# Reordering the first batch's front in an attention + token-mixing + MLP kernel on one Trainium2 core

## The chip, the cores and the metric

The kernel runs on one core of a Trainium2 chip. A core has a matrix engine (PE, with its weight loads shown apart as PEld), a vector engine (DVE), a scalar engine (ACT), a general engine (POOL), and a queue engine (SP) that here only issues DMAs. Each engine works through its own list of instructions in order and waits on semaphores for the others. Data lives in SBUF, and PE writes into eight PSUM banks of 128 x 512 f32. The metric is the time on the device of one execution in microseconds (us); lower is better. One execution was also recorded by the hardware profiler; all durations below are from that trace, counted from its start.

## The reference, cut to what matters

Chunked attention over B=4 batches, H=8 heads, S=768 tokens of D=64, then one block that mixes tokens with a low-rank pair U, V and channels with a two-layer MLP:

```python
def _attn_ref(q, k, v, mem_k, mem_v):            # chunk, left_ctx, right_ctx = 32, 16, 8; n_mem = 8
    for c in range(S // chunk):
        q_c = q[:, :, c*32 : c*32+32]
        k_full, v_full = memory rows + rows max(0, c*32-16) : min(S, c*32+40) of k, v
        scores = (q_c @ k_full.T) / sqrt(D)
        a = exp(scores - max);  a = a / (sum(a) + 1e-9)
        out[:, :, chunk] = a @ v_full

def _moe_ref(x, U, V, w_ch1, w_ch2):             # x: (4, 768, 512); U: (768, 32); V: (32, 768)
    h = x.transpose(0, 2, 1) @ U @ V
    u = x + h.transpose(0, 2, 1)
    return u + np.maximum(u @ w_ch1, 0.0) @ w_ch2   # w_ch1: (512, 2048), w_ch2: (2048, 512)
```

U, V, w_ch1 and w_ch2 arrive as float64, read on chip as pairs of 32-bit words.

## The kernel before

The kernel works batch by batch. A batch's attention runs in three parts, T = 0, 1, 2, each of 256 tokens: two token tiles `xs[(b, 2T)]` and `xs[(b, 2T+1)]` of 128 tokens x 512 channels. After attention the token mixing and the MLP of a batch run on PE in steps (`w1_step`, `w2_step`), and the next batch's attention is woven between them. Batch 0 has nothing to be woven into: its attention, the decoding of U, V and of the first slice of w_ch1 and the first half of its token mixing make up the **front**, roughly the first 47 us, and the first MLP step can't begin before it is over.

In the front the order of every engine's instructions is the order in which the Python code of `attention(0, ...)` writes them; a planner orders what comes later. Its pieces, with the line numbers of the profile:

- `q_part(T, h)` and `k_main(T, h, ...)` copy turned queries and keys into place on ACT (L694, L672 to L678). `s_turn(T)` makes a part's scores with 64 small matmuls (L714) in two banks.
- `s_weights(T)` takes, for each bank, the maximum (L736), the difference (L737), both on DVE, and the exponential on ACT (L740). `s_sums(T)` sums the rows (L745, two), adds 1e-9 (L749) and takes the reciprocal (L750), all on DVE: the normalization.
- `t_part(T, s)` turns the weights on PE (four matmuls, L768), and ACT copies them out of PSUM (L771). `av_part(T)` multiplies by v with 64 small matmuls (L788) into two banks, and DVE then writes the part's two token tiles with four products (L800).
- `collect(t)` adds U'x of token tile t to one PSUM bank, `gp[0]` (L812, one matmul with 512 columns in f32). `turn_x` turns token tiles 0, 1, 2 for all four column blocks (L1152, 12 matmuls) into four banks, two of the pool `ps_h` and the accumulators `acc0` and `acc1`. `turn_x1` does so later for tiles 3 to 5 (L1176).
- `Words` decodes float64 words: `begin` on ACT (L238), then `shift` (L245), `low` (L253, L258) and `join` (L265) on DVE. `u_words` is for U (its result goes to `u3` on DVE, L907, and to `u_sb` on POOL, L911), `v_words` for V. `spread_v` spreads V over partitions on PE (L290, 3 matmuls); ACT casts it (L295) and DVE subtracts (L296). `advance(5)`, behind it, decodes the first slice of w_ch1 (ACT L238; DVE L245 to L265), which therefore stands ahead of the last part's products L800 on DVE.
- `bank()` hands out PSUM banks in a cycle (`cyc`) over the pools `ps_a` (3 buffers), `ps_h` (2) and two accumulators while `wide[0]` is a number, and from `ps_a` alone once it is None. `keep_clock(n)` puts n matmuls of a zero tile `busy` (512 columns, L141) ahead of the next use of a bank; the program begins with 12 of them.
- `take(len(loading))`, behind `av_part(1)`, issues the loads of the last v rows and of the first slices of w_ch1 and w_ch2 on SP.

Of the kernel before, what the change touches and what calls it, by code (L numbers as in the profile page):

```python
# [25 lines left out]
HEAD = {ET.Activation, ET.Pool}  # L26
FIRST = 3000
START = 12
PROBS = [5, 0, 9]
LOADS = 'mv t1 t2 uv v0 v1 v2 a0 b0 w1 w2'  # L30
WLO = 4
# [27 lines left out]
def chunk_attn_then_mixer_kernel(  # L59
# [73 lines left out]
            return ps_h.tile([P, 512], F32, name="ps_h")  # L133
        return ps_o.tile([P, 512], F32, name="acc" + kind[1])

    warm = [0]

    def att_ps():
        ps = bank()
        for _ in range(warm[0]):  # L140
            nc.tensor.matmul(out=ps, lhsT=busy[:, 0:P], rhs=busy, start=True, stop=True)  # L141
        warm[0] = 0
        return ps

    def keep_clock(n):

        warm[0] += n

    busy = slot([P, 512], BF16, "busy")
    nc.vector.memset(busy, 0.0)  # L150
# [373 lines left out]
    def attention(b, xs):  # L524
# [141 lines left out]
        def k_main(T, h, psv):  # L666
            copy = nc.scalar.copy
            m, w = NM // 2, CK // 2
            kt = kall[:, NB * (T % 2):NB * (T % 2) + NB].rearrange("c i p (n r) -> c p r i n", r=2)
            for q_ in range(2):  # L670
                p = 2 * h + q_
                copy(out=kt[:, p, :, :, m:m + w], in_=psv[:, q_])  # L672
                copy(out=kt[:, p, :, 0:NB - 1, m + w:], in_=psv[:, q_, :, 1:, 0:NW // 2 - m - w])
            p = slice(2 * h, 2 * h + 2)
            if T == 0:
                copy(out=tail[:, p].rearrange("c p (n r) -> c p r n", r=2), in_=psv[:, :, :, 0, 0:LEFT // 2])
            if T == NP - 1:
                copy(out=kall[:, NB * (T % 2) + NB - 1, p, NM + CK:NM + CK + LEFT], in_=tail[:, p])  # L678
# [144 lines left out]
        if b == 0:  # L823
# [32 lines left out]
            take(1)  # L856
            spread_mv(vbs[0])
            take(2)
            keep_clock(START)
            regroup(kraw, kn, "kn", 0)  # L860
            for h in two:
                k_part(0, h)
# [25 lines left out]
            made = [k_edges(2, h) for h in two]  # L888
            for h in two:
                s_weights(0, *sc, [h])  # L890
                k_main(2, h, made[h])
            yield
            sc = s_turn(1)
            for h in two:
                q_part(2, h)
            s_weights(1, *sc)
            s_sums(0)
            u_words.begin()
            yield
            sc = s_turn(2)  # L900
            for s in two:
                t_part(0, s)
            s_weights(2, *sc)
            u_words.shift()
            u_words.low()
            av_part(0)
            nc.vector.tensor_copy(  # L907
                out=u3, in_=u_words.join()[:, 0:NT * R].rearrange("p (t r) -> p t r", t=NT)[:, :, None, :]
                .broadcast_to([P, NT, 3, R]),
            )  # L910
            nc.gpsimd.tensor_copy(out=u_sb, in_=u3[:, :, 0, :])  # L911
            s_sums(1)
            yield
            for s in two:
                t_part(1, s)
            v_words.begin()
            av_part(1)
            take(len(loading))
            for t in range(4):
                collect(t)  # L920
            s_sums(2)
            v_words.shift()
            v_words.low()
            val = v_words.join()
            for s in two:
                t_part(2, s)
            early = turn_x(range(NCK))
            wide[0] = None
            spread_v(val)
            yield  # L930
            advance(5)
            av_part(2)
            yield
            advance(1)
            for t in range(4, NT):
# [208 lines left out]

    def turn_x(cs):

        banks = []
        for c in cs:
            ps = ps_h.tile([P, 512], F32, name="ps_h") if c < 2 else ps_o.tile([P, 512], F32, name=f"acc{c - 2}")
            banks.append(ps)  # L1150
            for tt in range(TB):
                nc.tensor.matmul(  # L1152
                    out=ps[:, tt * P:(tt + 1) * P], lhsT=xs[(0, tt)][:, c * P:(c + 1) * P],
                    rhs=ident, start=(tt == 0), stop=False, skip_group_check=True,
                )
        return banks

    def join_uT(banks, g3):
        uht, ult = u_pair(0, 0)
# [562 lines left out]
```

## Time and profile before

| | us |
|---|---|
| median of 3 runs | 656.05 |
| the runs | 656.5, 656.05, 653.25 |
| the profiled execution | 653.21 |
| its span in the trace | 651.4 |
| PE busy | 620.5 (95% of the span) |
| DVE busy | 381.5 (59%) |
| ACT busy | 252.7 (39%) |

The profiled execution took 653.21 us, its trace spans 651.4 us, so 1.8 us lie outside the trace. The share of busy time is a mean over the whole program. The front has to be read from the timelines of PE, DVE and ACT, in which one row is a run of alike instructions: its start, how long it took, engine, line, operation, and in brackets how long the engine had been idle before it and what it waited for ("issue" means that the trace shows nothing that it waited for). A matmul of f32 data takes two passes, so it shows as two records.

### The profile page before, as it was taken

How to read it: one execution, taken by the hardware profiler on the slowest of the kernel's cores; microseconds unless marked ns; L12 is line 12 of the kernel's file. 1: busy time of each engine (PE TensorE's matmuls, PEld its weight loads, DVE VectorE, ACT ScalarE, POOL GpSimd, SP SyncE). 2: the span in 40 equal slices, each digit the busy share in tenths (PEclk: the TensorE clock that was granted, in tenths of full speed). 3: DMA queues.
4: the chain of work that ended last, by engine and by line, in shares of the span. 5: the costliest groups of instructions: out<-in, count | busy, mean ns of one | idle time of the engine just before them, and what ended most of it. 6: DMA issues, size and time to landing. Idle time of an engine off the chain costs nothing.

```text
span 651.4 us, 15085 instructions
## 1 busy us (share of the span) xinstructions
PE 620.5 (95%) x5992; PEld 537.0 (82%) x5992; DVE 381.5 (59%) x727; ACT 252.7 (39%) x635; POOL 139.2 (21%) x292
## 2 busy tenths in 40 slices
PE   7788999999898999899999999999999999999997
PEld 4557899988786889789889798898877899999886
DVE  6858788798792837953756824653546832222322
ACT  5426445348332445432245713321247712121221
POOL 5100000053153445302634200202315300000000
PEclk9989999999998999899999999999999999999999
DMA  9894586757886699576589949766413056555201
GB/s 244 156 352 176 172 252 226 226 179 177 177 191 163 162 309 297 182 183 157 170 246 206 173 149 263 242 180 181 138 46 116 1 169 187 145 165 160 97 1 48
DMA packets 168705, 115.02 MB, mean 177 GB/s; under 512 B 100956, under 2 KB 139484, under 8 KB 168636
## 3 DMA queue, kind: packets, MB, share of 16 engines
q1 hardware_dynamic: 168012, 113.92, 62.7%
q8 instruction: 47, 0.77, 0.5%
q10 hardware_dynamic: 624, 0.15, 0.1%
q14 instruction: 22, 0.18, 0.1%
HBM read 90.83 MB, written 28.97 MB: 184 GB/s over the span
## 4 chain that ended last, share of the span: by engine, by line
PE 56%; DVE 5%; DMA 3%; ACT 3%; POOL 2%; issue 2%; SPq 2%; ACTq 0%; DVEq 0%; POOLq 0%
PE ps_h L1322 23%; PE acc L1553 16%; PE acc L1563 8%; PE ps_a L788 2%; PE ps_h L1502 2%; DMA blocks<-spread 2%; ACT uc L169 1%; PE acc L1547 1%; DMA w1l<-w1s 1%; POOL pt L169 1%; PE ps_a L714 1%; PE ps_a L818 1%; POOL vb L493 1%; DVE x L1518 1%; DMA w1s<-vb 1%
## 5 line engine op out<-in xcount | busy, mean ns | idle before, releaser
L1553 PE MATMUL acc<-w,hh 128*128 128x512 f32 x612 | 158.3, 394 | 1.3 <-ACT hh L1336 1.3
L1553 PEld LDWEIGHTS acc<-w,hh 128*128 128x128 f32 x612 | 113.9, 189 | 23.1 <-ACT hh L1336 2.8
L1563 PE MATMUL acc<-w,hl 128*128 128x512 f32 x306 | 86.9, 392 | 0.0
L1563 PEld LDWEIGHTS acc<-w,hl 128*128 128x128 f32 x306 | 56.9, 188 | 11.9
L1322 PE MATMUL ps_h<-t12h,w1l 128*128 128x384 f32 x192 | 55.5, 343 | 1.0 <-ACT c L1348 0.7
L1322 PE MATMUL ps_h<-bh,w1l 128*128 128x384 f32 x192 | 53.6, 344 | 0.0
L169 POOL COPY pt<-y 32x128 f32<-32x128 f32 x96 | 30.2, 314 | 99.2 <-DVE y L166 95.0
L1322 PE MATMUL ps_h<-t34h,w1l 128*128 128x384 f32 x152 | 45.9, 343 | 0.2
L1502 PE MATMUL ps_h<-uh,w1h 128*128 128x384 f32 x124 | 42.9, 349 | 2.8 <-ACT w1h L395 1.7
L169 POOL COPY uc<-y 32x128 f32<-32x128 f32 x96 | 32.7, 340 | 56.2 <-DVE y L166 52.5
L1502 PE MATMUL ps_h<-ul,w1h 128*128 128x384 f32 x124 | 41.5, 339 | 0.4 <-DVE ul L1198 0.4
L1337 DVE SCALAR_TENSOR_TENSOR hl<-ps_h,hh 128x384 fp32r<-128x384 f32 x29 | 16.1, 554 | 42.8 <-ACT hh L1336 42.7
L1344 DVE TENSOR_TENSOR c<-ps_h,c 128x384 f32<-128x384 f32 x19 | 10.5, 554 | 48.8 <-PE ps_h L1322 48.8
L1322 PEld LDWEIGHTS ps_h<-t12h,w1l 128*128 128x128 f32 x192 | 35.2, 188 | 4.2 <-issue 1.4
L1337 DVE SCALAR_TENSOR_TENSOR hl<-hst,hh 128x384 fp32r<-128x384 f32 x36 | 20.6, 576 | 29.9 <-PE acc L1563 21.3
L1322 PEld LDWEIGHTS ps_h<-bh,w1l 128*128 128x128 f32 x192 | 35.6, 190 | 0.9 <-issue 0.2
L1322 PE MATMUL ps_h<-b,w1l 128*128 128x384 f32 x174 | 35.5, 339 | 0.3 <-DVE hst L1344 0.3
L1336 ACT ACTIVATE hh<-ps_h 128x384 fp32r<-128x384 f32 x29 | 14.2, 491 | 53.3 <-PE ps_h L1322 53.3
L1344 DVE TENSOR_TENSOR hst<-ps_h,hst 128x384 f32<-128x384 f32 x36 | 19.9, 553 | 24.0 <-ACT hst L1348 16.9
L1336 ACT ACTIVATE hh<-hst 128x384 fp32r<-128x384 f32 x36 | 18.8, 524 | 36.3 <-PE acc L1553 30.0
L1322 PE MATMUL ps_h<-t12l,w1l 128*128 128x384 f32 x96 | 32.3, 337 | 0.0
L575 POOL COPY kn<-kraw 128x512 f32<-128x512 f32 x8 | 8.3, 1039 | 112.5 <-DVE vb L258 102.2
(248 smaller groups left out, 1279.5 us busy)
## 6 DMA issues: line engine op xcount, KB each, us to landing
w1l<-w1s SPq DMA_DIRECT2D x155, 256.0 KB
rw<-in_moe_w_ch_dram SPq DMA_DIRECT2D x14, 512.0 KB
out_dram<-x SPq DMA_DIRECT2D x24, 256.0 KB
blocks<-spread SPq DMA_DIRECT2D x24, 256.0 KB
vb<-in_v_dram SPq DMA_DIRECT2D x56, 98.0 KB
raw<-in_moe_w_ch_dram SPq DMA_DIRECT2D x20, 256.0 KB
rw<-in_moe_w_ch_dram SPq DMA_DIRECT2D x16, 256.0 KB
w1s<-sums SPq DMA_DIRECT2D x16, 256.0 KB
```

Source lines behind the costliest of these rows:

```text
L169: (nc.scalar.copy if both and (5 * to + at) % 8 < 3 else nc.gpsimd.tensor_copy)(out=dst[CK * to:CK * to + CK, :, CK * at:CK * at + CK], in ...
L493: nc.gpsimd.tensor_tensor(out=out, in0=in0, in1=in1, op=op)
L575: (nc.gpsimd if b == 1 or front[0] and T == 2 else nc.vector).tensor_copy(out=groups[T, h].rearrange("n r h d -> n h r d"), in_=raws.pop(( ...
L714: nc.tensor.matmul(out=psv[s][(slice(CK * i, CK * i + CK), t) + ((p // 2, p % 2) if b >= DIRECT else (p % 2, p // 2))], lhsT=qt[p // 2][ro ...
L788: nc.tensor.matmul(out=psv[g][CK * i:CK * i + CK, t, j], lhsT=pt[s][rows, 2 * t + k_, CK * i:CK * i + CK], rhs=vt[rows, NI * t + i, D * j: ...
L1322: nc.tensor.matmul(out=ps[:, :TOK], lhsT=w_, rhs=u, start=(start and m == 0), stop=(m == 5), skip_group_check=True,)
L1336: nc.scalar.activation(out=hh, in_=c, func=AF.Relu)
L1337: nc.vector.scalar_tensor_tensor(out=hl, in0=c, scalar=0.0, in1=hh.bitcast(F32), op0=ALU.max, op1=ALU.subtract,)
L1344: nc.vector.tensor_tensor(out=out, in0=ps[:, :TOK], in1=in1, op=ALU.add)
L1502: nc.tensor.matmul(out=ph[:, :TOK], lhsT=w[:, c, :], rhs=u[c], start=(m == 0), stop=(m + 1 == len(parts)),)
L1553: nc.tensor.matmul(out=acc[tt], lhsT=h[:, sl], rhs=w, start=(begins and m == 0), stop=False,)
L1563: nc.tensor.matmul(out=acc[tt], lhsT=hl[:, sl], rhs=w2h[f], start=False, stop=ends is not None)
```

## The change

Nothing of what is computed changes. In the front of batch 0:

- `u_words.begin` moves on ACT from behind part 0's sums to between the exponential of part 0's first bank and `k_main(2, 0)`; the rest of U's decoding (DVE L245, L253, L258, L265, L907, POOL L911) moves from around `av_part(0)`'s products to behind part 0's two differences, ahead of part 1's first maximum.
- `v_words.begin` takes the place on ACT that `u_words.begin` leaves. The rest of V's decoding moves on DVE from behind part 2's sums to behind part 1's, ahead of `av_part(1)`'s products.
- The four collects 0 to 3, which stood together behind `av_part(1)`, are split: 0 and 1 ahead of `av_part(1)`, 2 and 3 behind it.
- `wide[0] = None` moves ahead of `t_part(2)`, so both of its banks are from `ps_a`.
- `turn_x` goes one token tile at a time (four matmuls): tile 0 ahead of `spread_v`, tile 1 behind it, tile 2 behind `av_part(2)`.
- `keep_clock` takes a width, and ten matmuls of the zero tile with 64 columns (FILL = 10) are put into the first bank of `av_part(2)` ahead of its own.

Lines of the changed kernel are one higher up to `attention`, and eight higher behind `turn_x`; within `attention` they differ by a few.

```diff
+FILL = 10
...
-    warm = [0]
+    warm = []
...
-        for _ in range(warm[0]):
-            nc.tensor.matmul(out=ps, lhsT=busy[:, 0:P], rhs=busy, start=True, stop=True)
-        warm[0] = 0
+        for width in warm:
+            nc.tensor.matmul(out=ps[:, 0:width], lhsT=busy[:, 0:P], rhs=busy[:, 0:width], start=True, stop=True)
+        warm.clear()
...
-    def keep_clock(n):
-        warm[0] += n
+    def keep_clock(n, width):
+        warm.extend([width] * n)
...
-            keep_clock(START)
+            keep_clock(START, 512)
...
             for h in two:
                 s_weights(0, *sc, [h])
+                if h == 0:
+                    u_words.begin()
                 k_main(2, h, made[h])
+            u_words.shift()
+            u_words.low()
+            nc.vector.tensor_copy(
+                out=u3, in_=u_words.join()[:, 0:NT * R].rearrange("p (t r) -> p t r", t=NT)[:, :, None, :]
+                .broadcast_to([P, NT, 3, R]),
+            )
+            nc.gpsimd.tensor_copy(out=u_sb, in_=u3[:, :, 0, :])
             yield
...
             s_sums(0)
-            u_words.begin()
+            v_words.begin()
             yield
...
             s_weights(2, *sc)
-            u_words.shift()
-            u_words.low()
             av_part(0)
-            nc.vector.tensor_copy(
-                out=u3, in_=u_words.join()[:, 0:NT * R].rearrange("p (t r) -> p t r", t=NT)[:, :, None, :]
-                .broadcast_to([P, NT, 3, R]),
-            )
-            nc.gpsimd.tensor_copy(out=u_sb, in_=u3[:, :, 0, :])
             s_sums(1)
             yield
             for s in two:
                 t_part(1, s)
-            v_words.begin()
-            av_part(1)
-            take(len(loading))
-            for t in range(4):
+            for t in two:
                 collect(t)
-            s_sums(2)
             v_words.shift()
             v_words.low()
             val = v_words.join()
+            av_part(1)
+            take(len(loading))
+            for t in two:
+                collect(2 + t)
+            s_sums(2)
+            wide[0] = None
             for s in two:
                 t_part(2, s)
             early = turn_x(range(NCK))
-            wide[0] = None
+            next(early)
             spread_v(val)
+            next(early)
             yield
             advance(5)
+            keep_clock(FILL, 64)
             av_part(2)
+            early = next(early)
             yield
...
     def turn_x(cs):
-        banks = []
-        for c in cs:
-            ps = ps_h.tile([P, 512], F32, name="ps_h") if c < 2 else ps_o.tile([P, 512], F32, name=f"acc{c - 2}")
-            banks.append(ps)
-            for tt in range(TB):
+        banks = [
+            ps_h.tile([P, 512], F32, name="ps_h") if c < 2 else ps_o.tile([P, 512], F32, name=f"acc{c - 2}") for c in cs
+        ]
+        for tt in range(TB):
+            for c in cs:
                 nc.tensor.matmul(
-                    out=ps[:, tt * P:(tt + 1) * P], lhsT=xs[(0, tt)][:, c * P:(c + 1) * P],
+                    out=banks[c][:, tt * P:(tt + 1) * P], lhsT=xs[(0, tt)][:, c * P:(c + 1) * P],
                     rhs=ident, start=(tt == 0), stop=False, skip_group_check=True,
                 )
-        return banks
+            yield banks
```

On PE, from the collects behind part 1 to those behind part 2, the kernel before has these rows (`acc_323` is the collects' bank, `dec` V's decoded words):

```order
L812 MATMUL acc_323<-x,uarea 96x512 x4
L768 MATMUL ps_a<-ident,pt 128x128 x4
L768 MATMUL ps_h<-ident,pt 128x128 x4
L1152 MATMUL ps_h<-ident,x 128x128 x6
L1152 MATMUL acc_845<-ident,x 128x128 x3
L1152 MATMUL acc_849<-ident,x 128x128 x3
L290 MATMUL ps_a<-dec,rep 96x256 x3
L788 MATMUL ps_a<-vbe,pt 32x64 x64
L812 MATMUL acc_323<-x,uarea 96x512 x2
```

All four collects, then all 12 turns of tokens (L1152), stand in one piece ahead of `spread_v` (L290). In the changed kernel the same stretch of PE, up to the first of the narrow matmuls, reads:

```order
L813 MATMUL acc_323<-x,uarea 96x512 x2
L769 MATMUL ps_a<-ident,pt 128x128 x8
L1160 MATMUL ps_h<-ident,x 128x128 x2
L1160 MATMUL acc_839<-ident,x 128x128
L1160 MATMUL acc_840<-ident,x 128x128
L291 MATMUL ps_a<-dec,rep 96x256 x3
L1160 MATMUL ps_h<-ident,x 128x128 x2
L1160 MATMUL acc_839<-ident,x 128x128
L1160 MATMUL acc_840<-ident,x 128x128
L142 LDWEIGHTS busy
L142 MATMUL ps_a<-busy 128x64
```

Two collects are gone from here to ahead of `av_part(1)`. Only four of the 12 turns of tokens are left ahead of `spread_v` (L290, now L291), four follow it, and behind them come the ten narrow matmuls (one pair of their rows is shown), `av_part(2)`, the last four turns and collects 4 and 5.

On DVE, from the last product of part 0 to the first two of part 1, the kernel before has (`dec` is here U's words, `pt` the weights, `rs` the reciprocal sums, `x` a token tile):

```order
L800 TENSOR_TENSOR x<-ps_a,rs 128x256
L265 TENSOR_TENSOR dec<-dec 128x192
L907 COPY uarea<-dec 128x576
L745 TENSOR_REDUCE rs<-pt 128x2x2x2 x2
L749 TENSOR_SCALAR rs<-rs 128x16
L750 RECIPROCAL rs<-rs 128x16
L800 TENSOR_TENSOR x<-ps_h,rs 128x256
L800 TENSOR_TENSOR x<-acc_727,rs 128x256
```

The sums (L745) stand behind U's last two steps. On DVE, in the same place, the changed kernel has (`dec` is now V's words, with `vraw` as their source):

```order
L801 TENSOR_TENSOR x<-ps_a,rs 128x256
L746 TENSOR_REDUCE rs<-pt 128x2x2x2 x2
L750 TENSOR_SCALAR rs<-rs 128x16
L751 RECIPROCAL rs<-rs 128x16
L246 TENSOR_SCALAR dec<-dec 96x256
L254 TENSOR_SCALAR dec<-dec 96x256
L259 SCALAR_TENSOR_TENSOR dec<-vraw,dec 96x256
L266 TENSOR_TENSOR dec<-dec 96x256
L801 TENSOR_TENSOR x<-ps_h,rs 128x256
L801 TENSOR_TENSOR x<-acc_733,rs 128x256
```

U's last two steps are gone from between part 0's products and part 1's sums, and V's four stand between those sums and part 1's products. On DVE of the changed kernel, from part 0's last difference to part 1's first maximum, stand:

```order
L738 TENSOR_TENSOR pt<-ps_a,mx 128x512
L246 TENSOR_SCALAR dec<-dec 128x192
L254 TENSOR_SCALAR dec<-dec 128x192
L259 SCALAR_TENSOR_TENSOR dec<-uarea,dec 128x192
L266 TENSOR_TENSOR dec<-dec 128x192
L897 COPY uarea<-dec 128x576
L737 TENSOR_REDUCE mx<-ps_a 128x8
```

Part 1's maximum (L736, now L737) now has U's five steps ahead of it on DVE. On the other engines the moves are those named above; the order of SP's DMAs is unchanged. Behind the front, in the first MLP steps, the order differs at one place on ACT: one Relu (L1510) stands ahead of the cast of the second slice of w_ch2 (L395) and three reads of words (L238), where it stood behind them.

## Rows read from the trace of the kernel before

**Rows 1.** Stretches: us, busy (count) of PE, PEld, DVE, ACT, POOL; clock, DMA share, GB/s.

```profile
0.00:14.00 14.00, 11.44 (x180) 7.38 (x181) 8.82 (x23) 6.77 (x25) 6.63 (x16) 1.00 0.93 260
30.00:35.00 5.00, 5.00 (x70) 2.76 (x59) 4.57 (x14) 0.38 (x1) 0.00 (x0) 1.00 0.79 208
44.00:45.00 1.00, 1.00 (x2) 0.28 (x1) 0.71 (x2) 0.00 (x0) 0.00 (x0) 0.50 1.07 393
80.00:90.00 10.00, 10.00 (x54) 9.24 (x53) 8.98 (x17) 3.23 (x7) 0.00 (x0) 1.00 0.78 242
```

**Rows 2.** Timeline of PE in the front: start, us, operation, idle before and releaser.

```profile
26.88 0.60 PE L768 MATMUL ps_a<-ident,pt 128*128 128x128 f32 x4
29.08 0.21 PE L788 MATMUL ps_h<-vb,pt 64*32 64x64 f32 x1 [0.95 <-issue]
30.48 3.67 PE L812 MATMUL acc<-x,uarea 128*96 128x512 f32 x8
33.99 0.60 PE L768 MATMUL ps_a<-ident,pt 128*128 128x128 f32 x4
34.86 1.82 PE L1152 MATMUL ps_h<-ident,x 128*128 128x128 f32 x12
37.95 0.68 PE L290 MATMUL ps_a<-dec,rep 32*96 32x256 f32 x6
39.58 1.75 PE L788 MATMUL ps_a<-vbe,pt 64*32 64x64 f32 x128 [0.94 <-issue]
43.51 3.64 PE L812 MATMUL acc<-x,uarea 128*96 128x512 f32 x4 [2.18 <-DVE x L800]
46.99 1.28 PE L1176 MATMUL ps_a<-ident,x 128*128 128x128 f32 x10
```

**Rows 3.** Timeline of DVE in the front.

```profile
17.88 0.69 DVE L736 TENSOR_REDUCE mx<-ps_a 128x8 f32<-128x512 f32 x1 [2.08 <-PE ps_h L714]
25.48 0.25 DVE L245 TENSOR_SCALAR dec<-dec 128x192 int32<-128x192 int32 x1
26.48 0.42 DVE L800 TENSOR_TENSOR x<-ps_h,rs 128x256 f32<-128x256 f32 x1
26.82 0.41 DVE L800 TENSOR_TENSOR x<-ps_a,rs 128x256 f32<-128x256 f32 x1
27.81 0.35 DVE L265 TENSOR_TENSOR dec<-dec 128x192 f32<-128x192 f32 x1
28.57 1.27 DVE L745 TENSOR_REDUCE rs<-pt 128x8 f32<-128x512 f32 x2
30.09 0.25 DVE L750 RECIPROCAL rs<-rs 128x16 f32<-128x16 f32 x1
33.58 0.23 DVE L245 TENSOR_SCALAR dec<-dec 96x256 int32<-96x256 int32 x1
34.63 0.42 DVE L265 TENSOR_TENSOR dec<-dec 96x256 f32<-96x256 f32 x1
39.06 1.09 DVE L296 TENSOR_TENSOR v<-ps_a,v 32x256 fp32r<-32x256 f32 x3 [4.01 <-ACT v L295]
42.70 1.42 DVE L800 TENSOR_TENSOR x<-ps_a,rs 128x256 f32<-128x256 f32 x4
```

**Rows 4.** Timeline of ACT in the front.

```profile
18.48 0.68 ACT L694 COPY qt<-ps_a 128x256 f32<-128x256 f32 x2 [0.61 <-PE ps_a L626]
21.19 0.37 ACT L238 ACTIVATE dec<-uarea 128x192 f32<-128x192 f32 x1
39.46 0.44 ACT L238 ACTIVATE dec<-rw 128x256 f32<-128x256 f32 x1
```

**Rows 5.** Timeline of PE: the zero tile's matmuls at the start.

```profile
1.47 4.97 PE L141 MATMUL ps_a<-busy 128*128 128x512 bf16 x12 [1.47 <-DVE kall L200]
```

**Rows 6.** Timeline of PE in the first MLP steps.

```profile
70.24 0.44 PE L1502 MATMUL ps_h<-uh,w1h 128*128 128x384 f32 x1 [0.56 <-ACT w1h L395]
```

**Rows 7.** A piece of the chain that ended last: start, us, what.

```profile
233.40 5.58 DMA blocks<-spread
```

## The prediction

> **What bounds the kernel now.** I read the page first: PE is busy for 95% of the span, so a gain has to come from PE's own idle time or from PE running slowly. The table by stretches came second. In a typical later stretch PE is busy for 10.00 of 10 us [rows 1]. There nothing can be won, but a lead that PE brings into such a stretch is also kept. So I turned to PE's timeline in the front and looked for the brackets, which are the idle times.
>
> The end of the front hangs on a loop between PE and DVE. PE makes weighted values of part 2 at 39.58, but the collects 4 and 5 start only at 43.51, after 2.18 us idle, waiting for DVE's products [rows 2]. DVE's products begin at 42.70 [rows 3], though PE had the values ready from 39.58+1.75 = 41.33 on. DVE was late because it had the subtractions of spread V and w_ch1's words to do first, and before those it sat idle for 4.01 us until PE had spread V [rows 3]. PE spread V at 37.95, behind 12 turns of tokens (34.86 to 37.95) and four collects [rows 2], although V's words had been joined by 34.63+0.42 = 35.05 [rows 3]. So the path is: collects, turns of weights, turns of tokens, spread of V, V's subtractions, w_ch1's words, products, collects. The reader is to see that DVE's queue order makes PE's order at 34 us set the time at 43 us.
>
> A second loss sits at the same place. Collects 4 and 5 take 46.99 - 43.51 = 3.48 us, the four before them 33.99 - 30.48 = 3.51 us [rows 2], so one costs 1.74 instead of 0.88. In that stretch the granted clock is 0.50 [rows 1], the 1.2 GHz level; PE had been idle for 0.94 us, busy for 1.75 and idle for 2.18 before it [rows 2].
>
> **U's words, moved ahead.** They are five steps of DVE, 26.48 - 25.48 = 1.00 us for three and 28.57 - 27.81 = 0.76 for two, together 1.76. They now stand ahead of part 1's first maximum, where DVE sat idle for 2.08 us waiting for scores [rows 3]. They fit with 0.32 to spare, if U has landed. Ahead of U on its queue lie 12 loads of q and k of 256 KB; with U's own 192 KB that makes 3.34 MB. The first 14 us moved 260 GB/s, or 3.64 MB [rows 1], so I estimate that U is there at about 13 us; the latest the trace allows is 21.19, when ACT read it [rows 4]. On ACT the read (0.37) now stands ahead of `k_main(2)`. ACT has 0.61 idle before its next copies of q [rows 4], so this is free, and ACT's old place is filled by V's read of about the same length. POOL's copy of u_sb is small and nothing in the front reads it. What is won is that part 1's sums come 0.76 earlier. The other 1.00 lay ahead of part 0's products, where it may have covered nothing but PE's matmuls: part 1's turns come behind those on PE and were at their second bank at 26.88 [rows 2], so the products at 26.48 [rows 3] could hardly have begun sooner. I take nothing for it.
>
> **Collects 0 and 1 ahead of `av_part(1)`.** The turns of part 1's weights end at 26.88 + 0.60 = 27.48 [rows 2], and token tile 0 is complete at 26.82 + 0.41 = 27.23 [rows 3]. Two collects of 0.88 run from 27.48 to 29.24. Before, `av_part(1)` stopped for 0.95 us with no cause that the trace names and went on at 29.08 [rows 2]. Part 2's same 64 matmuls without such a stop took 1.75 [rows 2]; from 29.24 they end at 30.99. I take it that the stop, which came at a place in PE's instruction stream and not at a wait, passes while the collects run; if it doesn't, it costs 0.95 (rival B).
>
> By the Trainium skill ("Runtime: NRT & Kernel Launch", Instruction fetch mechanics) PE's instructions are streamed in blocks of 256 and the crossing of a block is mostly hidden. The 0.95 us row, with no other releaser, speaks against "hidden" for such small matmuls, but not against a stop that overlaps long ones. Were the page right, the stop would be `av_part(1)`'s own and the sum would be that of rival B.
>
> **V's words ahead of part 1's products.** Part 1's sums now start at 27.81 and take 30.09 + 0.25 - 28.57 = 1.77, to 29.58. V's four steps take 34.63 + 0.42 - 33.58 = 1.47 [rows 3], to 31.05, 0.06 behind PE's 30.99. So V's words are nearly free here, but their cover is only this thick: each 0.1 that they are longer is 0.1 on the path. Products follow each other by 0.34 (26.48 to 26.82) and take 0.41 [rows 3]; tile 2 is complete at 31.05 + 0.34 + 0.41 = 31.80. PE idles 0.81 us for it, a new wait. Collects 2 and 3 then end at 31.80 + 1.76 = 33.56, against 33.99 [rows 2]: **0.43 won**, no more.
>
> **Turns of tokens, spread out.** The turns of part 2's weights keep their 0.87 (33.99 to 34.86), to 34.43; the second bank from `ps_a` waits for nothing, since ACT has copied the first bank out before `spread_v` needs it. Of the 12 turns (37.95 - 34.86 = 3.09) a third, 1.03, stays ahead of `spread_v`, which starts at 35.46 instead of 37.95 [rows 2]: **2.49 won** in all up to here, 2.06 of it from the turns. V's cast and subtractions, w_ch1's words and the last products on DVE are one unbroken chain behind it, so products begin at 42.70 - 2.49 = 40.21 and the first collect at 43.51 - 2.49 = 41.02. ACT would read w_ch1's words at 39.46 - 2.49 = 36.97 [rows 4]. They were issued at 30.7 to 32 behind what was left of v; 208 GB/s from 30 to 35 us [rows 1] make 1.0 MB, about twice their 0.5 MB, so I estimate that they are there.
>
> What cover does this use up? PE does tile 1's turns from 35.46 + 0.68 = 36.14 to 37.17. `av_part(2)`'s first bank is free at 39.58 - 2.49 = 37.09. With 1.75 for it and 1.03 for tile 2's turns PE is through at 39.95, before 41.02. So these turns cost nothing, and 1.07 us is left for the narrow matmuls.
>
> **Ten narrow matmuls.** No row has this form. The cheapest near one is a matmul of `av_part(2)`, 1.75/128 = 0.014 us; the dearest is the zero tile's own with 512 columns, 4.97/12 = 0.41 [rows 2, 5]. Ten cost 0.14 to 4.1 us. Columns are an eighth of the dear ones' 512, so I stand near the low end, at 0.5, inside the 1.07: free. At the upper end 3.1 us would stick out.
>
> The Trainium skill ("TensorE: Matmul & The Clock Gate", Back-to-back issue gap) gives a measured 81 ns for each pair of weight load and 128-column matmul; by that the ten would be an estimated 0.8 us at most, also free. No run here shows it.
>
> **The clock.** Where PE had idled 0.94 and then 2.18 us, it now idles 0.81 early, and between tile 2's turns and collect 4 about 41.02 - 39.95 - 0.5 = 0.6. I take it that the clock stays at 2.4 GHz. Collects 4 and 5 then take 1.76 instead of 3.48: **1.72 won**. They end at 42.78 against 46.99.
>
> **The sum.** 2.49 + 1.72 = 4.21. Behind the front the change is one Relu that ACT does earlier; PE's idle 0.56 there [rows 6] is the most it could give, and about as much is what a Relu early in the queue could cost, so zero, ±0.56. The profiled execution's 653.21 becomes 649.0. Of four executions (profiled one included) two lie at 653.2 and two at 656.05 to 656.5; from the latter the same 4.21 leaves 651.8. The median of before is 656.05, 2.84 above the profiled one, and the median after may fall at either level; I take the middle, **650.4**.
>
> **Rivals.** A, the clock falls all the same, since the idle 0.81 and 0.6 are still there: collects at 1.74, 1.72 given back, 650.7 to 653.6. For it: the idle times don't vanish. Against: the 0.95 us stop before 29.08 left the clock at 1.00 in the stretch from 30 us [rows 1, 2]; it was low only behind the 2.18. B, the stop in `av_part(1)` isn't hidden: it ends at 31.94, 0.89 behind V's words, 649.9 to 652.7. C, the lead is lost downstream: the chain of waits has stretches that hang on transfers, one of 5.58 us [rows 7], and if that transfer isn't itself earlier, PE waits longer for it: 653.2 to 656.05, no change. For it: 5.58 is more than 4.21. Against: what issues it runs behind PE's steps, so it should move too. D, slower: U lands late, and part 1's maximum waits on DVE behind U's words for ACT's read. With U landing at L the maximum starts at L + 0.37 + 1.76 instead of 17.88, and all of part 1 and 2 with it. This eats the gain when L = 15.75 + 4.21 = 19.96; at the latest possible 21.19 it is 5.44 late, the time 654.4, 1.2 slower than the profiled execution; with narrow matmuls at the dear price 657.5. Against it: the estimate of 13 us.
>
> **How the numbers follow.** Forecast 0.62, A 0.13, B 0.08, C 0.12, D 0.05. A measurement of this kernel tells about 0.5%, 3.3 us, from no change: under 652.8 is faster, over 659.3 slower. The forecast is faster at either level, though at 651.8 with little room, so 0.56 of its 0.62 count as faster; half of A (0.06) and of B (0.04) too. Sum 0.66 faster. The rest of these, C and most of D are no change, 0.31. D with the dear matmuls at the upper level leaves 0.03 slower. The range goes from 647.5 (649.0 less the 0.56, and less one more stop like the 0.95 that the new order may happen to cover) to 654.5, which takes in A, B, half of C and D's 654.4.
>
> **What would show it.** `spread_v` near 35.5 and the first late collect near 41.0; late collects of 0.88 each at a granted clock of 1.00; no idle of DVE ahead of part 1's maximum but 0.3; ten narrow matmuls of under 1.07 together. If the late collects take 1.74 it is A; if a stop of about 0.95 stands inside `av_part(1)`, B; if the front ends near 42.8 and the end is still at 651, C; if part 1's maximum starts past 18, D. I would be wrong altogether if the front's chain ran through something else than V's spread, such as w_ch1's words landing after 37.

## The result, and the profile after

The changed kernel takes 645.33 us (median of 6 runs, 641.1 to 649.09) against 655.27 us for the kernel before (6 runs, 653.25 to 656.5): a ratio of 0.985, 95% interval 0.981 to 0.990. All ratios here are taken without the runs over 1.5% above the fastest of their kernel (among them single ones of 858.3 and 994.67 us), so they can differ a little from the quotient of the medians beside them. The changed kernel is about 10 us faster, where 5.7 were forecast for the median (656.05 to 650.4), and below the range's lower end of 647.5. Its profiled execution took 641.1 us, the fastest of the six, with a span of 639.2.

The front came out nearly as worked out. PE's timeline of the changed kernel, in the columns of [rows 2]:

```profile
32.16 1.96 PE L813 MATMUL acc<-x,uarea 128*96 128x512 f32 x4 [1.28 <-DVE x L801]
33.96 1.04 PE L769 MATMUL ps_a<-ident,pt 128*128 128x128 f32 x8
35.82 0.68 PE L291 MATMUL ps_a<-dec,rep 32*96 32x256 f32 x6
37.42 0.46 PE L142 MATMUL ps_a<-busy 128*128 128x64 bf16 x10
41.38 1.96 PE L813 MATMUL acc<-x,uarea 128*96 128x512 f32 x4 [0.59 <-DVE x L801]
43.17 2.17 PE L1184 MATMUL ps_a<-ident,x 128*128 128x128 f32 x18
45.10 0.59 PE L1169 MATMUL ps_h<-v,g 96*128 96x384 f32 x2
```

V's spread moved from 37.95 [rows 2] to 35.82, the collects 4 and 5 from 43.51 to 41.38, and they now take 43.17 - 41.38 = 1.79 instead of 3.48. The front ends at 43.17 instead of 46.99, 3.82 earlier. But the span shrank by 651.4 - 639.2 = 12.2, so 8.4 us were won behind the front, where the forecast had zero. The stretches show two places of it, first the kernel before, then the changed one at the same work, which it reaches 7 to 12 us earlier (columns of [rows 1]):

```profile
195.00:215.00 20.00, 17.68 (x201) 13.39 (x200) 7.37 (x16) 4.33 (x10) 6.63 (x9) 0.91 0.73 192
440.00:460.00 20.00, 19.10 (x339) 17.06 (x338) 8.47 (x21) 4.35 (x9) 4.37 (x15) 1.00 0.62 166
```

```profile
188.00:208.00 20.00, 19.66 (x221) 15.21 (x220) 9.94 (x23) 6.56 (x15) 9.42 (x13) 1.00 0.85 222
428.00:448.00 20.00, 20.00 (x347) 18.15 (x346) 9.53 (x23) 5.00 (x10) 5.21 (x18) 1.00 0.61 166
```

In the kernel before PE loses 2.3 us in the first stretch and runs part of it at the low clock (0.91 on average); in the changed kernel it loses 0.34, at the full clock. PE's timeline names the idle times behind it, all in runs of small matmuls that multiply by v (L788, in the changed kernel L789), the kernel before first, then the changed one:

```profile
200.93 0.43 PE L788 MATMUL ps_a<-vb,pT 64*32 64x64 f32 x6 [2.31 <-issue]
448.08 0.33 PE L788 MATMUL ps_a<-vb,pT 64*32 64x64 f32 x12 [0.90 <-issue]
```

```profile
194.06 0.35 PE L789 MATMUL ps_a<-vb,pT 64*32 64x64 f32 x16 [0.33 <-issue]
```

These stops are of the kind of the 0.95 in [rows 2]: nothing that PE waits for, in a run of small matmuls. The DMA view of the kernel before, from 198.5 to 200.0 us, where the stop of 2.31 lies (198.62 to 200.93), has an instruction packet in it, and the page counts these packets (queue and kind: packets, MB, share of the DMA engines):

```profile
q8 instruction: 1, 0.02, 5.1%
```

```profile
q8 instruction: 47, 0.77, 0.5%
```

The page has 5992 matmul records and 5992 weight loads of PE; 11984/47 makes 255, so a packet holds about 256 of PE's instructions (0.77 MB/47 is 16 KB). Ten narrow matmuls are 20 instructions, and they move every later end of a packet by 20 instructions against the program. That gave **theory 1**: the 20 instructions moved the ends of the packets away from where they hurt in batch 1's and batch 2's values. **Theory 2**: the earlier front alone changed what falls together far behind it, and the narrow matmuls have no part in it.

### The profile page after: what moved, and what is told of

Its sections match the earlier page's. It is cut to its first block, busy times and chain, and to the rows that moved or that the text cites. A ratio compares the mean times of both kernels' runs of the same rounds, so it can differ in the third digit from the quotient of the medians.

```text
span 639.2 us, 15107 instructions
## 1 busy us (share of the span) xinstructions
PE 616.1 (96%) x6002; PEld 534.6 (84%) x6002; DVE 382.2 (60%) x727; ACT 252.2 (39%) x635; POOL 138.1 (22%) x292
## 4 chain that ended last, share of the span: by engine, by line
PE 69%; DVE 9%; DMA 7%; SPq 5%; ACT 5%; issue 3%; POOL 2%; ACTq 0%; DVEq 0%; POOLq 0%
PE ps_h L1330 24%; PE acc L1561 18%; PE acc L1571 9%; PE ps_h L1510 7%; PE ps_a L789 2%; DMA blocks<-spread 2%; SPq L609 2%; ACT uc L170 1%; PE acc L1555 1%; PE ps_a L715 1%; PE ps_a L1561 1%; DMA rw<-in_moe_w_ch_dram 1%; DMA w1l<-w1s 1%; DVE vb L259 1%; POOL pt L170 1%
## 5 line engine op out<-in xcount | busy, mean ns | idle before, releaser
L1510 PE MATMUL ps_h<-uh,w1h 128*128 128x384 f32 x124 | 42.5, 347 | 2.2 <-ACT w1h L396 1.1
L1510 PE MATMUL ps_h<-ul,w1h 128*128 128x384 f32 x124 | 41.3, 337 | 0.4 <-DVE ul L1206 0.4
L1356 ACT COPY c<-ps_h 128x384 f32<-128x384 f32 x19 | 9.1, 479 | 59.0 <-PE ps_h L1330 59.0
```

Source lines behind the costliest of these rows:

```text
L1356: nc.scalar.copy(out=out, in_=ps[:, :TOK])
L1510: nc.tensor.matmul(out=ph[:, :TOK], lhsT=w[:, c, :], rhs=u[c], start=(m == 0), stop=(m + 1 == len(parts)),)
```

## The experiments

All timed runs are compared with the kernel before on their chip. Single executions of one kernel scatter more than the three runs shown at first: the kernel before ran between 646.8 and 660.2 in 35 runs on one chip. So the medians of several runs, and stops counted over many profiles, carry the argument.

### Take the narrow matmuls away, put them in alone, put them elsewhere

The changed kernel without them:

```diff
-FILL = 10
+FILL = 0
```

> The changed kernel without its ten narrow matmuls; all else as changed. The front of the changed kernel ended at 43.17 us (start of the turns behind collects 4 and 5), before it was 46.99. Theory 1 (the 20 instructions of the narrow matmuls move the places at which PE's instruction packets end, and with them the stops far behind the front): front at 42.7 to 43.4 if the clock holds, 44.9 if it falls; the stops of before at about 200 us (2.31) and 448 us (0.90) come back, each some 4 us earlier, and with the first the low clock behind it; the median is 649 to 652. Theory 2 (the earlier time alone makes the stops go): median as the changed kernel, 643 to 648, no such stops in the profile. If the narrow matmuls hold the clock at collects 4 and 5, these take 3.5 us together, else 1.8.

Measured: 652.13 us against 654.23, ratio 0.999 (0.996 to 1.003). Its front is as early as the changed kernel's (collects 4 and 5 at 41.68, at the full clock, the next step at 43.48), but the stops are there:

```profile
41.68 1.96 PE L813 MATMUL acc<-x,uarea 128*96 128x512 f32 x4
43.48 2.17 PE L1184 MATMUL ps_a<-ident,x 128*128 128x128 f32 x18
...
198.72 0.31 PE L789 MATMUL ps_a<-vb,pT 64*32 64x64 f32 x6 [3.42 <-issue]
419.48 0.34 PE L789 MATMUL ps_a<-vb,pT 64*32 64x64 f32 x15 [1.53 <-issue]
446.59 0.33 PE L789 MATMUL ps_a<-vb,pT 64*32 64x64 f32 x12 [1.21 <-issue]
```

So the narrow matmuls aren't needed for the clock at the collects, and without them most of the gain is gone. This speaks against theory 2: the front is early, and the stops stay.

The kernel before with ten narrow matmuls ahead of `av_part(2)` and nothing else:

```diff
             advance(5)
+            keep_clock(10, 64)
             av_part(2)
```

> The kernel before with ten narrow matmuls of 64 columns ahead of part 2's values and nothing else of the change. Theory 1 (instruction places): front as before, 47.0 (or 45.3 if they hold the clock); the stops at 200 us and 448 us change, the low clock near 200 us goes, median 648 to 651. Theory 2 (earlier time): nothing changes but at most 1.7 us for the clock, median 653 to 656.

Measured: 650.25 us, ratio 0.996 (0.992 to 1.0005); no stop of over 0.7 us near 195, 418 or 445 us, though the front is nearly as late as before (collects 4 and 5 at 43.05, next step at 45.82). Theory 1's side, at the edge of what the interval can tell.

The changed kernel, and the kernel before, with 11 narrow matmuls in the warm-up at the start in place of one wide one:

```diff
-            keep_clock(START, 512)
+            keep_clock(START - 1, 512)
+            keep_clock(FILL, 64)
...
-            keep_clock(FILL, 64)
             av_part(2)
```

> The changed kernel with the narrow matmuls taken from ahead of part 2's values to the warm-up at the start (11 of them, for one wide one: again 20 instructions more in all). Theory 1: what follows the front is as in the changed kernel, median 643 to 648; theory 2 the same. Against the run without any narrow matmuls it parts the two: theory 1 puts it 4 to 6 us below, theory 2 level with it. The collects 4 and 5 show whether the narrow matmuls hold the clock: 3.5 us together if they were needed there, else 1.8.

> The kernel before with 11 narrow matmuls for one wide one of the warm-up, 20 instructions more, no other change; the front stays within 0.3 of 47.0 and its low clock stays. Theory 1: the stops at about 200 and 448 us change and the median falls by 3 to 6, to 649 to 652. Theory 2: median 654 to 656, stops as before.

Measured: 653.73 us, ratio 1.000 (0.996 to 1.0045), and 651.57 us, ratio 0.997 (0.9935 to 1.0006). The first is a miss for both theories as they were written: the same 20 instructions, but no gain. The profiles tell why. Put ahead of the whole front, they move the packets' ends inside the front too. In the changed kernel so altered a stop of 2.02 stands in `av_part(1)`, in the altered kernel before one of 2.18:

```profile
34.47 0.24 PE L789 MATMUL acc<-vb,pt 64*32 64x64 f32 x1 [2.02 <-issue]
47.73 1.96 PE L813 MATMUL acc<-x,uarea 128*96 128x512 f32 x4 [1.09 <-DVE x L801]
```

```profile
33.27 0.31 PE L788 MATMUL acc<-vb,pt 64*32 64x64 f32 x1 [2.18 <-issue]
48.45 1.96 PE L812 MATMUL acc<-x,uarea 128*96 128x512 f32 x4 [2.18 <-DVE x L800]
```

Collects 4 and 5 start at 47.73 and 48.45, some 5 to 6 us later than in the changed kernel and the kernel before; behind the front both are free of the far stops near 200, 418 and 445 us. The place of the narrow matmuls, behind part 1's values, matters.

### A whole packet more, and a packet and 20 instructions

```diff
-FILL = 10
+FILL = 128     (and, in the other run, 138)
```

> The changed kernel itself, unaltered, beside the next three on their chip, so that they can be compared with it. Both theories: median 643 to 648, no stop near 195 us in the profile, front at 43.2.

> The changed kernel with 128 narrow matmuls in place of ten: 256 instructions of PE, one whole instruction packet (the trace of before holds one such packet for every 256). At 0.046 us each (0.46 for ten in the changed kernel's trace) they add about 5.4 to the front, which ends near 48.6. Theory 1 (the place within the packet counts): the same places as with no narrow matmuls, so the stop of 2.3 to 3.4 us in batch 1's values comes back, at about 204 us. Theory 2 (an earlier time makes it go): this run and the next have lost the lead alike, so both have the stop. Median 655 to 659 by either.

> The changed kernel with 138 narrow matmuls: 256 + 20 instructions, so by theory 1 the same places in the packets as the changed kernel's ten, though the front is as late as with 128 (near 49.1). Theory 1: no stop of over 1 us in batch 1's values near 200 us, and 3 to 5 us faster than the run with 128: median 650 to 654. Theory 2: a stop as with 128, and 0.5 slower than it.

Measured: the changed kernel itself 644.82 us, ratio 0.988 (0.982 to 0.994), with a stop of 0.60 at 195.18 and the front's end at 43.81. With 128 it took 656.56 us, ratio 1.002 (0.998 to 1.006); with 138, though its front ends later still, 651.75 us, ratio 0.997 (0.994 to 1.0002). Both fronts ended some 3 us later than expected, at 51.53 and 52.05, behind stops of 3.12 and 3.21 in `av_part(2)`. The stretch from 195 to 215 us, 128 first, then 138:

```profile
195.00:215.00 20.00, 16.32 (x194) 12.77 (x194) 7.95 (x18) 3.96 (x9) 10.32 (x13) 0.83 0.64 156
```

```profile
195.00:215.00 20.00, 19.99 (x222) 15.56 (x222) 10.12 (x22) 5.49 (x13) 10.86 (x14) 1.00 0.80 214
```

128 narrow matmuls are 256 instructions, a whole packet (both pages count 48 packets, against 47 before): the ends fall as with none, and PE loses 3.68 us there and the full clock. Ten matmuls more, and it loses nothing. These two rows alone prove little, since a stop near 200 us also comes in some profiles with the ends moved (below). The medians of 12 runs each carry the argument: 4.8 us between two kernels that are alike in all but 20 instructions, and the one with the later front is the faster. Theory 2 can't give that.

### Which part of the reordering makes the front

The turns of tokens split by tile (with `wide[0] = None` ahead of `t_part(2)`) and nothing else; then the words and collects moved and nothing else:

```diff
+            wide[0] = None
             for s in two:
                 t_part(2, s)
             early = turn_x(range(NCK))
-            wide[0] = None
+            next(early)
             spread_v(val)
+            next(early)
             yield
             advance(5)
             av_part(2)
+            early = next(early)
```

> The kernel before with only the turns of tokens split by tile (and part 2's second bank from the other pool), no narrow matmuls, words and collects as before. By the prediction's terms the turns are 2.06 of the 2.49 won in order, and the shorter idle ahead of collects 4 and 5 keeps the clock (1.72): front ends at 43.2 to 43.6. If words and collects are needed for the clock, 44.9 to 45.3. Behind the front the packets are as before, so by theory 1 the stop near 200 us stays; median 650 to 654.

> The changed kernel with the turns of tokens and part 2's banks as before and no narrow matmuls: only U's and V's words and the collects are moved. The run with the turns alone already ended the front at 43.20, as early as the whole change (43.17), so the words and collects should add nothing by themselves: front at 46.5 to 47.0, clock low at collects 4 and 5, median within 2 of before. The prediction's terms for them, 0.43 in all, say 46.6. If they are what the turns need, the front is at 45 or less.

Measured: 651.37 us, ratio 0.997 (0.993 to 1.0001), and 653.1 us, ratio 0.999 (0.995 to 1.002). Turns alone (first three rows), words and collects alone (last two):

```profile
30.48 3.67 PE L812 MATMUL acc<-x,uarea 128*96 128x512 f32 x8
41.41 1.96 PE L812 MATMUL acc<-x,uarea 128*96 128x512 f32 x4 [0.93 <-DVE x L800]
43.20 2.17 PE L1179 MATMUL ps_a<-ident,x 128*128 128x128 f32 x18
```

```profile
44.20 1.96 PE L813 MATMUL acc<-x,uarea 128*96 128x512 f32 x4 [2.18 <-DVE x L801]
46.00 2.17 PE L1180 MATMUL ps_a<-ident,x 128*128 128x128 f32 x18
```

With collects 0 to 3 at 30.48 as in the kernel before [rows 2], the split turns bring collects 4 and 5 to 41.41, 2.10 earlier, where the whole change has 41.38. The words and collects leave them at 44.20, against 43.51 before [rows 2]; two profiles of the kernel before differ by more than that (43.51 and 45.06), so the sign isn't shown, but a gain isn't there either. What that run wins in the front, it wins by the clock, which was expected to be low: its collects take 1.80, behind the same 2.18 of idle time that stood ahead of the slow ones in the kernel before. The far stops agree with the expectation only in part: with the turns alone there is 0.43 near 200 us instead of a long stop, but 2.32 at 417.61 and 0.90 at 444.45; with words and collects alone there is none over 0.5.

### The two parts that work, together

The turns with ten, and with 20, narrow matmuls, words and collects as before; and the whole change with 20:

```diff
             advance(5)
+            keep_clock(10, 64)     (and, in another run, 20)
             av_part(2)
+            early = next(early)
...
-FILL = 10
+FILL = 20
```

> The kernel before with the turns of tokens split and the ten narrow matmuls, words and collects as before. If those two parts make the whole gain, it equals the changed kernel: front near 43.2, no stop of over 1 us near 195, 415 and 440 us, median 643 to 648, ratio 0.983 to 0.990. If words and collects matter, 648 to 652.

> The changed kernel with 20 narrow matmuls in place of ten. The idle ahead of collects 4 and 5 (0.59) covers their added 0.46, so the front stays within 0.2 of 43.2. What changes is the place in the packets, by 20 instructions more: by theory 1 the stops far behind the front may differ from those of the changed kernel, so the median may be anything from 642 to 652; by theory 2 it is that of the changed kernel, 643 to 648.

> The kernel before with the turns split and 20 narrow matmuls; words and collects as before. If words and collects are worth nothing measurable, it equals the changed kernel with 20 (ratio 0.9853 to the kernel before, interval 0.9811 to 0.9895). If they are worth their terms in the prediction (0.43) or more, 0.986 to 0.992.

Measured: 648.61 us, ratio 0.989 (0.986 to 0.993), for turns and ten; 643.54 us, ratio 0.985 (0.981 to 0.9895), for the whole change with 20 (front's end at 43.62); 644.54 us, ratio 0.984 (0.9805 to 0.987), for turns and 20. The first lies between the two expectations, at the edge of both, and its profile was a poor one (PE waited 2.21 us for a v row in the front and 3.79 us at 201.79). The last two can't be told apart, nor from the changed kernel's 0.985: the moved words and collects have no measurable share.

### U's words and POOL's copy

One step of U's words takes 1.83 us on DVE in the changed kernel instead of 0.26. The copy of the memory values on POOL is written behind U's words instead of ahead:

```diff
-            spread_mv(vbs[2])
-            take(2)
...
             nc.gpsimd.tensor_copy(out=u_sb, in_=u3[:, :, 0, :])
+            spread_mv(vbs[2])
+            take(2)
             yield
```

> The changed kernel with POOL's copy of the memory values into part 2's home (1.9 us long) written behind U's words instead of ahead of them. In every trace of the changed words one of U's steps on DVE takes 1.83 us and ends just behind that copy, against 0.26 before. If the copy holds the step up, the step now takes 0.25 to 0.45, part 1's first maximum starts near 17.8 instead of 19.2, and the front ends up to 1 us earlier, 42.2 to 43.2. If the step is slow for another reason (waiting for U's load), it stays at 1.8.

DVE and POOL in the changed kernel, then with the copy moved:

```profile
16.12 1.83 DVE L254 TENSOR_SCALAR dec<-dec 128x192 int32<-128x192 int32 x1
19.22 0.68 DVE L737 TENSOR_REDUCE mx<-ps_a 128x8 f32<-128x512 f32 x1
...
15.92 1.93 POOL L843 COPY vbe<-mv 128x2048 f32<-128x2048 f32 x1
```

```profile
16.88 0.26 DVE L254 TENSOR_SCALAR dec<-dec 128x192 int32<-128x192 int32 x1
18.49 0.68 DVE L737 TENSOR_REDUCE mx<-ps_a 128x8 f32<-128x512 f32 x1
...
18.92 1.90 POOL L843 COPY vbe<-mv 128x2048 f32<-128x2048 f32 x1
```

The step is held up until POOL's copy ends (15.92 + 1.93 = 17.85, the step's end 17.95) and takes 0.26 when the copy comes later. The Trainium skill ("SBUF — State Buffer", Who interferes with whom) says that GpSimd and DVE share a pair of ports, that tensor_scalar can take it when its operands meet certain conditions, and that whoever issues first holds the pair for the whole instruction while the other is fully blocked. The trace agrees: POOL's copy began at 15.92, the step at 16.12, and it took 1.83 against 0.26. The time didn't move, though: 644.59 us, ratio 0.987 (0.983 to 0.991), and the front ended at 43.33. The front's gain that was expected didn't come; the products of that profile stood behind a stop of 1.50 in `av_part(0)`, so an earlier DVE there only waited for PE.

### How often the stops come

A further profile each of the kernel before, of the change without narrow matmuls and of the changed kernel:

> The kernel before, profiled a second time. Of five profiles with its places in the packets (before, no narrow matmuls, 128 narrow ones, turns only, words and collects only) three have a stop of 2.3 to 3.7 us near 200 us and three one of 0.9 to 1.2 near 445 us. If the places in the packets set the odds of these stops and the moment of each execution draws them, this one has at least one of the two, and a low clock at collects 4 and 5 (3.5 us together), or at another stop of the front. If the first profile was a single bad draw, none.

> The changed kernel without narrow matmuls, profiled a second time. If its places in the packets set the odds: a stop of over 0.7 us near 196, 418 or 445 us, as in its first profile (3.42, 1.53 and 1.21); front near 43.5 at full clock in collects 4 and 5. If those stops were a single draw, none.

> The changed kernel, profiled a third time. None of nine profiles with 20 or 40 instructions more has a stop near 418 or 445 us, and two of nine have one of over 2 us near 200. Expected: none near 418 and 445, most likely none near 195; front 43.1 to 43.9.

Measured, in one execution each: 658.24, 649.79 and 648.77 us. In the first, collects 4 and 5 took 47.25 - 45.06 = 2.19 us, between the two levels of the clock, and the low clock lasted into the turns behind them. The fronts of the other two ended at 44.84 and 44.19, later than expected. The stops of the kernel before in its second profile, and of the change without narrow matmuls in its second; then the only far stop of the changed kernel in its third, which was not expected:

```profile
203.70 0.43 PE L788 MATMUL ps_a<-vb,pT 64*32 64x64 f32 x6 [3.31 <-issue]
424.83 0.34 PE L788 MATMUL ps_a<-vb,pT 64*32 64x64 f32 x15 [1.71 <-issue]
453.33 0.33 PE L788 MATMUL ps_a<-vb,pT 64*32 64x64 f32 x12 [1.01 <-issue]
```

```profile
417.35 0.34 PE L789 MATMUL ps_a<-vb,pT 64*32 64x64 f32 x15 [1.84 <-issue]
444.46 0.33 PE L789 MATMUL ps_a<-vb,pT 64*32 64x64 f32 x12 [1.17 <-issue]
```

```profile
197.98 0.47 PE L789 MATMUL ps_a<-vb,pT 64*32 64x64 f32 x16 [3.02 <-issue]
```

All 18 profiles, by the place of the packets' ends. "Rest" is the span less the start of the first join of the tokens' mix (L1161 before, L1169 in the changed kernel: 48.91 and 45.10), so it leaves the front out:

| instructions added to PE | profiles | stop near 200 (over 2 us) | near 418 (over 1.5) | near 445 (0.9 or more) | rest, mean (range) |
|---|---|---|---|---|---|
| 0 or 256 | 7 | 4 | 4 | 5 | 602.5 (597.8 to 606.0) |
| 20, 40 or 276 | 11 | 3 | 0 | 0 | 597.6 (594.1 to 600.8) |

Near 418 and 445 us the two groups part clearly; near 200 us, 4 of 7 against 3 of 11 doesn't tell them apart. The traces also show the stops at their place. Counting all of PE's records in order (matmuls, weight loads, its semaphore instructions), 63 of the 67 idle times of 0.6 us or more that have no releaser, in all 18 traces, stand at the same place in their count of 256 (remainder 193 or 194; the other four are the 0.94 ahead of `av_part(2)` [rows 2]). The 19 of them behind the front end 1.1 to 1.5 us after an instruction packet has landed. What the moved ends change is how early that packet comes. Near 418 us it landed 4.3 to 7.4 us ahead of PE's reaching that place in all 11 profiles with moved ends, near 445 us 6.2 to 6.6. In the five other profiles that stopped at 445 us it landed 1.2 to 1.5 ahead of PE's going on at either place, and in the two that didn't stop, 3.2 to 4.0. Near 200 us it is 1.1 to 1.5 in all 18, so there PE is on the edge in either group.

The 20 instructions go with 4.9 us less behind the front on average. Stops of 0.5 us or more make about half of it (3.6 us in a profile against 1.2); the rest, to which the low clock that may follow a stop belongs, isn't split up further. In the joins' starts themselves the kernel before has 48.91 and 50.42, the changed kernel 45.10, 45.74 and 46.12: 49.7 to 45.7, or 4.0 us for the front. Together 8.9, against 9.9 between the medians. One part alone is worth less in time than its share of this: by the ratios the early front without narrow matmuls gave 0.001 and 0.003 (whole change, turns alone), the ten alone 0.004, and both together 0.011 to 0.016. No run explains the difference.

## Why the prediction was wrong

The step that failed is the one behind the front: "Behind the front the change is one Relu that ACT does earlier ... so zero, ±0.56", with the sentence ahead of it that a lead brought into a full stretch is simply kept. I priced the narrow matmuls by their time alone. The same document had a stop of 0.95 in its rows, and I called it a place in PE's instruction stream; I didn't draw from it that 20 more instructions move all such places behind them. That term is 4.9 us on average and 8.4 in the profiled execution. The size in that execution was luck in part: it had no long stop near 200 us, where the changed kernel's third profile has one of 3.02. It isn't only a gain: it might as well have gone the other way, as the runs with the narrow matmuls at the start show for the front. The Trainium skill ("Runtime: NRT & Kernel Launch", Instruction fetch mechanics) calls the crossing of a block mostly hidden; stops of 2.31 and 3.68 us in runs of small matmuls disagree, while at the place near 418 us, where the packet had landed 4.3 us or more ahead, PE indeed lost nothing.

Point by point:

- **What bounds the front** was right. V's spread was forecast at 35.46 and came at 35.82; the first late collect at 41.02 and came at 41.38; the front's gain was forecast at 4.21, and is 3.82 in the first profile and 4.0 between the means. The 0.39 that the first profile lacks come from the words and collects.
- **Turns of tokens, spread out**: mechanism and size were right, 2.10 measured with the turns alone against 2.06. They are the whole of what the new order won, not 2.06 of 2.49.
- **V's words and collects 0 to 3**: 0.43 was forecast; in the changed kernel part 2's weights are turned from 33.96 on, against 33.99 before [rows 2], so 0.03 came of it. The stop in `av_part(1)` did hide behind collects 0 and 1 in the changed kernel, but PE then waited 1.28 us for tile 2 instead of the 0.81.
- **U's words**: 1.76 was to fit into an idle time of 2.08. One step took 1.83 by itself, and part 1's first maximum came at 19.22 instead of 17.88 [rows 3]. The load of U was there in time; rival D's cause wasn't the one at work, but its place was. I had looked at POOL's copy of u_sb and not at the 1.9 us copy beside U's words.
- **Ten narrow matmuls**: 0.5 was taken, 0.46 measured, and covered. That they keep the clock isn't shown: the change without them has its collects at full clock in both its profiles (43.48 - 41.68 = 1.80 in the first), and in the kernel before with the ten alone they took 45.82 - 43.05 = 2.77, partly at the low clock.
- **The clock**: full in all three profiles of the changed kernel at collects 4 and 5. But the idle time that I made answerable doesn't decide it by itself, since after the same 2.18 us the words-and-collects run kept the full clock. So 1.72 is what the fall cost the profiled execution, not what every execution pays.
- **The Relu behind the front**: PE's wait of 0.56 [rows 6] is gone in all three profiles of the changed kernel, the most that I had allowed it to give.
- **The median**: I set two of four executions at each of two levels and took the middle. With more runs the kernel before spreads from 647 to 660 without a gap, so there are no two levels.

What stays open: where the packet lands only 1.1 to 1.5 us ahead of PE, as near 200 us, the stop is anything from none to 3.8 us long from one execution to the next, and no run here shows what decides it, nor why the two parts of the change gain more together than each alone. The best of the kernels, turns with 20 narrow matmuls and the whole change with 20, aren't clear of the changed kernel itself.

## What to carry to other kernels

Where a profile shows PE stopping with no releaser in runs of small matmuls, count PE's instructions: a few instructions added or taken away ahead can be worth more, for better or worse, than the step that they belong to, and an edit has to be compared with a version of equal instruction count before its gain is put down to its idea. In a chain that passes between two engines, look for work that stands ahead of the hand-over and isn't needed by it; splitting such a block by tile was the whole of the front's gain here.

## What the runs showed of the hardware

PE's instruction packets (47 in the span, about 256 instructions each) can stop it for up to 3.8 us in runs of small matmuls; behind the front PE goes on 1.1 to 1.5 us after a packet has landed. Moving the packets' ends by 20 or 40 instructions left no stop near 418 and 445 us in all 11 profiles, where five of the other seven have stops of 0.9 to 2.3 us. A DVE step on data in SBUF stood still for 1.83 instead of 0.26 us until a POOL copy ended. And the granted clock doesn't follow one idle time: 2.18 us of idle led to the 1.2 GHz level at the kernel before's collects (3.48 us), and not in the run with words and collects alone (1.80 us).
